# Batch 0's attention of the state rows as a separate pass between batches 2 and 3 of a fused attention, MLP and MoE kernel

## The chip, the cores and the metric

The kernel runs on one NeuronCore of a Trainium2 chip. The metric is the device time of one execution in microseconds (us). The engines are TensorE (PE, matrix products), VectorE (DVE), ScalarE (ACT), GpSimd (POOL) and SyncE (SP, whose queue issues most DMA transfers and DMA transposes). Each engine works its own queue of instructions in order, so an instruction that waits holds up everything behind it on that engine.

## What is computed

Three stages follow each other. The first is an attention between 512 token rows and 32 state rows, for 8 batches and 8 heads, in both directions. The results of a batch (512 + 32 rows of 8 x 64 columns) are laid side by side to 4608 tokens of 512 columns, and these go through an MLP and then through a mixture of 8 experts of which each token takes one.

```python
# x: [8, 8, 512, 64], state: [8, 8, 32, 64]   (batch, head, row, column)
scores  = x @ state.T / 8
xread   = softmax(scores) @ state              # the 512 token rows
scores2 = state @ x.T / 8
sread   = softmax(scores2) @ x                 # the 32 state rows
x = concatenate([xread, sread], rows)          # 4608 x 512

h = x @ w_in                                   # 512 x 2048
x = (maximum(h, 0) ** 2) @ w_out               # 2048 x 512

expert = argmax(x_normed @ emb_normed.T / tau) # one of 8
out = gate * (maximum(x @ w1[expert], 0) @ w2[expert])   # 512 x 1024 x 512
```

`w_in` and `w_out` come as fp64 and are turned into fp32 on the chip; all other inputs and the output are fp32.

## The kernel before

**Precision.** Most fp32 products are made of three fp16 products: each factor is split into a high part and the rest (`split`, `splits`: a scaled copy on ACT, L331, and a subtraction on DVE, L317). A scale for each matrix comes first, from sums of squares. Batch 0's score products, and the first products with `w_in`, are taken in fp32, before any scale is known.

**Work units.** The token rows of batch b are two units of 256 tokens, u = 2b and 2b + 1, and all state rows together are the last unit, u = 16. `w_in` has eight blocks of columns, c = 0 to 7. The MLP's first product uses that xread is a weighted sum of state rows: for each batch, `state_w` (L674, for batch 0 `first_state_w`) makes `sw` = state x `w_in` once, in four steps k = 0 to 3 of two PSUM banks `S0` and `S1` (pool `ps_s`, one of each), and `up1` multiplies the transposed attention weights `aT` with `sw` into a tile `u` of PSUM (L1388 to L1390, twelve products a unit and block with two units side by side; two buffers). `hidden` reads `u` on ACT (L1341) and goes on to `g`, and `down1` multiplies `g` with `w_out` into `d` (L1472 to L1474).

**The token side of the attention.** `attention(b)` waits for x and the state of its batch, for the end of batch b - 1, and for the tile of the splits. It takes squares (L463, L465), makes scales and splits of x and the state, and the scores. `weigher` then makes the softmax, writes it in halves (the cast L544 on ACT, the subtraction on DVE) and asks SP for the transpose into `aT` (L553), one for each unit. Batch 0 has functions of its own: `first_attention`, `first_scores` (fp32 products, L604) and `first_scale` (the scale of x).

**The state side.** `state_side(b)` makes the scores of the state rows (L756; fp32 products for batch 0, three fp16 products for the others), the maxima (L763), two exps (L768), the splits of the exps into `he`, a transpose of `he` through SP (L779), two splits of `xS` (L331), 48 closing products (L800 to L802), and the two halves `x8_h` (L810, two instructions) and `x8_l` of its columns of unit 16. It ends with `ev("att", b)`, on which batch b + 1 waits. For batch 0 it is started by `first_scale`, and it has two waits of its own: for the scale of x (`"first sx"`), and at L772 for a step of the weights' preparation:

```python
GATE_S = ('wosq', 3)
...
        if b == 0:
            yield ev(*GATE_S)
```

**Buffers and loads.** x comes twice per batch: as `xT` (columns first, for scores) and as `xS` (rows first, for the closing products). Both use one buffer of 1 MB (`xf_slots`), the state has one buffer (`st_slots`), the halves one (`xhl_slots`), and the exps with their transposes one (`eb_slots`). All four are single, and lie in the tiles that the trace calls `xx`, `stt`, `xx` and `he`. `loader` brings the batches in turn, each load as soon as the buffer is free:

```python
        yield from load_x(0, 1)
        for b in range(1, B):
            yield from load_st(b)
            yield from load_x(b, 0)
            yield from load_x(b, 1)
```

**What sets the order.** No scheduler runs on the chip. At build time a planner (`Plan`) holds a list of threads (Python generators such as `attention(b)`, `state_side(b)`, `loader`), each with a priority. A thread yields an engine and an estimated duration, an event, or a buffer. The planner takes the thread that can start first (with the priority, a lower number first, where they tie) and writes its instructions into the engine's queue. So a change in a thread, in a wait or in a priority shifts the order of all engines behind it.

**The early stage.** While batches 0 and 1 go through attention, the weights `w_in` and `w_out` are loaded, turned into fp32 (first step on ACT, L908), squared (ACT L940, L999) and split (`wi`, ACT L986; `wo_t`, ACT L1047). Later, while the MLP runs over batches 1 to 7, the experts' weights are loaded, split and stored as `w_d`, 2 MB for each load of the MoE stage. That stage starts behind the MLP (L1688 loads, L1782 to L1784 first products).

Of the kernel before, what the change touches and what calls it, by code (L numbers as in the profile page):

```python
# [41 lines left out]
BW = DFF // NB  # L42
GATE_S = ('wosq', 3)
BLOCKS = [(kind, 2 * k + i) for k in range(NB // 2) for kind in "io" for i in range(2)]
# [9 lines left out]
PRIO_A1 = 1.25  # L54
PRIO_S0 = 1.1
XE = 2
SMALL = 2
# [188 lines left out]
def moe_kernel(  # L246
# [154 lines left out]
    def ev(*key):  # L401
        return evs.setdefault(key, Ev(plan))
# [19 lines left out]
    def load_st(b):  # L422
        yield st_slots
        stt = att.tile([128, 4, 64], F32, name="stt")
        t = yield from load(stt, stT[b], 128 * 1024)
        st_t[b] = stt
        ev("st", b).set(t)

    def load_x(b, which):
        yield xf_slots  # L430
        t = xf_v
        xf_t[b, which] = t
        if b or which:
            ev("x", b, which).set((yield from load(t, (xT, xS)[which][b], 1 << 20)))
        else:
            for i in range(2):
                q = slice(256 * i, 256 * i + 256)
                ev("first x", i).set((yield from load(t[:, :, q], xT[0][:, :, q], 1 << 19)))

    def loader():  # L440
        yield ev("raw", LOADER)
        yield from load_x(0, 1)
        for b in range(1, B):
            yield from load_st(b)
            yield from load_x(b, 0)
            yield from load_x(b, 1)
# [5 lines left out]
    def attention(b):  # L452
        yield ev("x", b, 0)
        yield ev("st", b)
        xf, stt = xf_t.pop((b, 0)), st_t.pop(b)
        yield ev("att", b - 1)
        yield xhl_slots
# [106 lines left out]
    def first_attention():  # L564

        yield ev("st", 0)
        stt = st_t.pop(0)
        yield xhl_slots
        xh, xl = halves_tile()
        ss = small.tile([128, 3], F32, name="ss")  # L570
        yield act(256)
        nc.scalar.activation(out=xl.bitcast(BF16)[:, :, :64], in_=stt, func=AF.Square, accum_out=ss[:, 2:3])
        yield t_slots
        p = ps_t.tile([128, 512], F32, name="t")
        yield "pe", 0.2
        mm(p[:, 2:3], lhsT=one32, rhs=ss[:, 2:3], start=True, stop=True)
        mm(p[:, 256:512], lhsT=oneb, rhs=xl.bitcast(BF16)[:, :, :64], start=True, stop=True)
        for t in range(2):
            plan.add(first_scores(t, xh, xl, stt), 0.4 + 0.1 * t)
        plan.add(first_scale(ss, stt), 0.95)  # L580
        v = small.tile([128, 2], F32, name="sv")[:, 0:1]
        yield tiny(4)
        V.tensor_scalar(out=v, in0=p[:, 2:3], scalar1=FLOOR, scalar2=None, op0=ALU.max)
        pow2(sx[:, 1:2], isx[:, 1:2], v, 204)
        yield sth_slots
        sthl = att.tile([128, 2, 4, 64], F16, name="sthl")
        stf = sthl.rearrange("p a c n -> p (a c n)").bitcast(F32).rearrange("p (c n) -> p c n", c=4)
        yield dve2(256)
        V.tensor_scalar(out=stf, in0=stt, scalar1=sx[:, 1:2], scalar2=float(2.0 ** -14), op0=ALU.mult, op1=ALU.mult)
        plan.add(first_state_w(stf), 0.6)  # L590
        plan.add(group_bound(0, p), 0.7)

    def first_scores(t, xh, xl, stt):
# [5 lines left out]
        Sp, k_h = ps_u.tile([128, 512], F32, name="u").rearrange("p (a n) -> p a n", a=2), u_slots.last()  # L599
        yield "pe", 3.4  # L600
        for a in range(2):
# [8 lines left out]
    def first_scale(ss, stt):  # L610

        for t in range(2):
            yield ev("scored", t)
        xf = xf_t.pop((0, 0))
        plan.add(state_side(0, ((stt, xf),), eighth), PRIO_S0)
        for i in range(2):
# [3 lines left out]
            nc.scalar.activation(out=jk, in_=xf[:, 2 * i:2 * i + 2], func=AF.Square, accum_out=ss[:, i:i + 1])  # L620
            pjk_slots.release()
        at = plan.now()
        yield t_slots
# [9 lines left out]
        pow2(sx[:, 0:1], isx[:, 0:1], v, 204)  # L633
        ev("first sx").set()
        for C in range(2):
            yield ev("ST", 0, C)
        xf_slots.release()
# [101 lines left out]
    def state_side(b, pairs, scl):  # L739
# [9 lines left out]
        for C in range(2):  # L749
            yield t_slots  # L750
            plan.cur[2] = max(at, plan.now())
            p = ps_t.tile([128, 512], F32, name="t")
            yield "pe", 0.8 if b else 1.7
            for n, (a, x) in enumerate(pairs):
# [6 lines left out]
        for C, p in enumerate(ps):  # L761
# [8 lines left out]
            t_slots.release()  # L770
        if b == 0:
            yield ev(*GATE_S)  # L772
        yield tiny(3)
# [7 lines left out]
        yield ev("x", b, 1)  # L781
        if b == 0:
            yield ev("first sx")
        xs = xf_t.pop((b, 1))
        yield xhl_slots
        xsh, xsl = halves_tile()
        sxb = sx[:, 2 * b:2 * b + 1]
        yield from splits([(xsh[:, q], xsl[:, q], xs[:, q], sxb) for q in (slice(0, 2), slice(2, 4))], 1024)
# [16 lines left out]
        pov = po[:, 0:256].rearrange("p (c i n) -> p c i n", c=4, i=2)  # L805
        ns = slice(b * NS, b * NS + NS)
        qs = [(i, slice(64 * i, 64 * i + 64)) for i in range(2)]
# [1061 lines left out]
    def start():  # L1869
# [6 lines left out]
        for b in range(1, B):  # L1876
            plan.add(attention(b), 1.15 if b == 1 else PRIO_A1)
        plan.add(loader(), 1)
# [51 lines left out]
```

## Time and profile before

| | us |
|---|---|
| median of 3 runs | 1085.97 (1083.8 to 1086.14) |
| the profiled execution | 1084.85 |
| its span, from the first to the last instruction | 1083.1 |
| PE busy | 1040.1 (96% of the span) |
| DVE busy | 666.7 (62%) |
| ACT busy | 590.3 (55%) |
| POOL busy | 121.6 (11%) |

The granted clock of PE is 0.987 of its full rate as a mean over the span. The MoE stage's first products start at 689.52 us. To read such a profile: busy shares say which engine is full over the whole span, but stages differ, so a table of stretches comes next. The list of waits says what ended the idle time in front of an instruction. A timeline gives the start of each instruction on one engine, its duration, and in brackets the idle time before it with what ended it. Starts of instructions that follow each other at once lie closer together than the durations, since they overlap in the engine.

### The profile page before, as it was taken

Reading aid. Unit: us, or ns where it says so; the run is one execution under the profiler, and the core shown is the slowest. Engines: PE = TensorE matmul, PEld = TensorE weight load, DVE = VectorE, ACT = ScalarE, POOL = GpSimd, SP = SyncE. Lnnn points to the kernel's source line nnn. Section 1 sums busy time; section 2 is a strip of 40 time slices with the busy share of each in tenths; the row PEclk is TensorE's granted clock in tenths of the full one; section 3 lists DMA queues with packets and bytes.
Section 4 is the critical chain, followed back from the end, with each engine's and each line's share of the span. In section 5 each row is a group of like instructions: output and inputs, shape, how many; then the busy total and the mean of one; then the engine's idle time right before and its main releaser. Section 6 shows DMA issues by size and latency. Waiting matters only on the chain. (4 is left out here: it accounts for less than half of the span.)

```text
span 1083.1 us, 26144 instructions
## 1 busy us (share of the span) xinstructions
PE 1040.1 (96%) x10521; PEld 669.9 (62%) x10521; DVE 666.7 (62%) x1817; ACT 590.3 (55%) x990; POOL 121.6 (11%) x149
## 2 busy tenths in 40 slices
PE   5989999999999999999999999999999999999988
PEld 4445555565565665655656566677767667776764
DVE  6779888878878788788876864465233222222222
ACT  6999988878878789778768773111111101011110
POOL 0000000102001001010020200321121122121101
PEclk9889999999999999999999999999999999999999
DMA  9854567676674867667377677935986766875690
GB/s 298 326 169 146 124 199 168 187 196 175 167 204 149 184 163 233 165 196 215 79 224 223 213 252 270 230 89 148 301 236 167 214 174 198 230 226 151 207 294 30
DMA packets 161311, 211.73 MB, mean 195 GB/s; under 512 B 112225, under 2 KB 115041, under 8 KB 155938
## 3 DMA queue, kind: packets, MB, share of 16 engines
q1 hardware_dynamic: 152434, 182.86, 58.9%
q0 software_dynamic: 8320, 27.08, 7.8%
q8 instruction: 84, 1.38, 0.5%
q14 instruction: 41, 0.34, 0.1%
q10 hardware_dynamic: 432, 0.08, 0.0%
HBM read 257.92 MB, written 51.68 MB: 286 GB/s over the span
## 5 line engine op out<-in xcount | busy, mean ns | idle before, releaser
L1738 ACT ACTIVATE r<-u 128x512 f32<-128x512 f32 x70 | 41.8, 597 | 327.6 <-PE u L1784 300.2
L1474 PE MATMUL d<-wo_t,g 128*128 128x512 f16 x480 | 181.9, 379 | 1.4 <-DVE g L1360 1.4
L1472 PE MATMUL d<-wo_t,g 128*128 128x512 f16 x480 | 181.9, 379 | 0.8 <-DVE g L1358 0.8
L1473 PE MATMUL d<-wo_t,g 128*128 128x512 f16 x480 | 181.9, 379 | 0.0
L1388 PE MATMUL u<-aT,sw 128*128 128x256 f16 x512 | 141.2, 276 | 13.0 <-ACT sw L666 5.5
L1390 PE MATMUL u<-aT,sw 128*128 128x256 f16 x512 | 140.9, 275 | 0.7 <-DVE sw L317 0.7
L1389 PE MATMUL u<-aT,sw 128*128 128x256 f16 x512 | 141.0, 275 | 0.2 <-issue 0.2
L1741 DVE CAST hh<-r 128x512 f16<-128x512 f32 x70 | 30.1, 430 | 139.4 <-ACT r L1738 137.8
L1341 ACT ACTIVATE r<-u,cg 128x512 f32<-128x512 f32 x120 | 81.8, 684 | 50.7 <-PE u L1390 32.3
L1752 DVE TENSOR_SCALAR o<-d,rec,wo_t 128x512 f32<-128x512 f32 x35 | 28.3, 810 | 109.8 <-PE d L1807 103.0
L1314 POOL DMA_INDIRECT rec_d<-rec,pi x34 | 38.1, 1119 | 483.0 <-DVE g L1360 111.2
L1807 PEld LDWEIGHTS <-hh 128*128 128x128 f16 (+1 forms) x688 | 54.9, 103 | 58.0 <-issue 2.0
L1360 DVE TENSOR_TENSOR g<-r,g 128x512 f16<-128x512 f32 x120 | 82.2, 688 | 7.6 <-ACT r L1355 6.1
L1474 PEld LDWEIGHTS <-g 128*128 128x128 f16 x480 | 47.0, 98 | 58.7 <-DVE g L1360 1.9
L1783 PE MATMUL u<-xes,stage 128*128 128x128 f16 x448 | 76.0, 219 | 0.0
L1784 PE MATMUL u<-xes,stage 128*128 128x128 f16 x448 | 76.0, 219 | 0.0
L1782 PE MATMUL u<-xes,stage 128*128 128x128 f16 x448 | 76.0, 219 | 0.0
L1355 ACT ACTIVATE r<-r 128x512 f32<-128x512 f32 x120 | 74.6, 626 | 1.2
L1472 PEld LDWEIGHTS <-g 128*128 128x128 f16 x480 | 47.1, 98 | 45.4 <-DVE g L1358 1.3
L1388 PEld LDWEIGHTS <-sw 128*128 128x128 f16 x512 | 51.3, 100 | 37.6 <-issue 17.3
L1473 PEld LDWEIGHTS <-g 128*128 128x128 f16 x480 | 47.0, 98 | 44.0
L1782 PE MATMUL u<-xes,xx 128*128 128x128 f16 x416 | 70.5, 219 | 0.0
(331 smaller groups left out, 2610.1 us busy)
## 6 DMA issues: line engine op xcount, KB each, us to landing
w_d<-he SPq DMA_DIRECT2D x128, 256.0 KB
g<-w_d SPq DMA_DIRECT2D x16, 2048.0 KB
wo_t<-w_d SPq DMA_DIRECT2D x16, 2048.0 KB
stage<-w_d SPq DMA_DIRECT2D x14, 2048.0 KB
he<-w_d SPq DMA_DIRECT2D x14, 2048.0 KB
xx<-w_d SPq DMA_DIRECT2D x13, 2048.0 KB
sw<-w_d SPq DMA_DIRECT2D x13, 2048.0 KB
stage<-in_w_dram SPq DMA_DIRECT2D x21, 1024.0 KB
```

The source lines that it names most:

```text
L1341: nc.scalar.activation(out=r, in_=ps, func=AF.Relu, scale=cg[:, g:g + 1] if u >= F32U else cgq[:, c:c + 1])
L1355: nc.scalar.activation(out=r, in_=r, func=AF.Square)
L1360: V.tensor_tensor(out=gl, in0=r, in1=gh, op=ALU.subtract)
L1388: mm(o, lhsT=hl[:, i, 0, fs], rhs=aT[:, i, :], start=i == 0, stop=False)
L1389: mm(o, lhsT=hl[:, i, 0, fs], rhs=aT[:, 2 + i, :], start=False, stop=False)
L1390: mm(o, lhsT=hl[:, i, 1, fs], rhs=aT[:, i, :], start=False, stop=i == 1)
L1472: mm(ps, lhsT=g_h[:, f, ts], rhs=w[:, 0, :], start=f == 0, stop=False)
L1473: mm(ps, lhsT=g_h[:, f, ts], rhs=w[:, 1, :], start=False, stop=False)
L1474: mm(ps, lhsT=g_l[:, f, ts], rhs=w[:, 0, :], start=False, stop=f == KF - 1)
L1782: mm(p[:, j, xs], lhsT=w[:, 0, k, fs], rhs=xe[:, k, xs], start=k == 0, stop=False)
L1783: mm(p[:, j, xs], lhsT=w[:, 0, k, fs], rhs=xe[:, 4 + k, xs], start=False, stop=False)
L1784: mm(p[:, j, xs], lhsT=w[:, 1, k, fs], rhs=xe[:, k, xs], start=False, stop=k == 3)
```

## The change

The state side of batch 0 no longer runs with the rest of batch 0. A new thread `late_side` runs it as a pass of its own with the number B = 8, at the fourth place of a list ATT = (0, 1, 2, 8, 3, ..., 7). Its parts:

- `loader` goes through ATT. `xT` and the state of batch 0 are loaded a second time for the pass (index `b % B`), and `xS` of batch 0 is loaded then and not early. The first load behind batch 0's `xT` is now the state and `xT` of batch 1.
- `first_scale` frees x and the state of batch 0 once the squares are made, and starts no state side. A new event `"stf"` says that the scaled state has been written, since the state's buffer may go only then.
- `attention(b)` waits for the pass ahead of it in ATT. Batch 1 waits for no other batch. Its priority goes from 1.15 to 1.0. Batch 3 now waits for the late pass, and the late pass for batch 2.
- The two waits that `state_side` had for batch 0 go away. The late pass still uses fp32 score products (1.7 us in the planner instead of 0.8).
- The planner's estimate for the first score products goes from 3.4 to 3.2 us.

```diff
-GATE_S = ('wosq', 3)
+ATT = (0, 1, 2, B, 3, 4, 5, 6, 7)
...
-        t = yield from load(stt, stT[b], 128 * 1024)
+        t = yield from load(stt, stT[b % B], 128 * 1024)
...
-            ev("x", b, which).set((yield from load(t, (xT, xS)[which][b], 1 << 20)))
+            ev("x", b, which).set((yield from load(t, (xT, xS)[which][b % B], 1 << 20)))
...
         yield ev("raw", LOADER)
-        yield from load_x(0, 1)
-        for b in range(1, B):
+        for b in ATT[1:]:
             yield from load_st(b)
             yield from load_x(b, 0)
             yield from load_x(b, 1)
...
     def attention(b):
...
-        yield ev("att", b - 1)
+        if b > 1:
+            yield ev("att", ATT[ATT.index(b) - 1])
...
         V.tensor_scalar(out=stf, in0=stt, scalar1=sx[:, 1:2], scalar2=float(2.0 ** -14), op0=ALU.mult, op1=ALU.mult)
+        ev("stf").set()
...
-        yield "pe", 3.4
+        yield "pe", 3.2
...
     def first_scale(ss, stt):
...
         for t in range(2):
             yield ev("scored", t)
+        yield ev("stf")
+        st_slots.release()
         xf = xf_t.pop((0, 0))
-        plan.add(state_side(0, ((stt, xf),), eighth), PRIO_S0)
...
             pjk_slots.release()
+        xf_slots.release()
...
         ev("first sx").set()
+
+    def late_side():
+
+        yield ev("x", B, 0)
+        yield ev("st", B)
+        xf, stt = xf_t.pop((B, 0)), st_t.pop(B)
+        yield ev("att", ATT[ATT.index(B) - 1])
+        plan.add(state_side(B, ((stt, xf),), eighth), PRIO_S0)
         for C in range(2):
-            yield ev("ST", 0, C)
+            yield ev("ST", B, C)
         xf_slots.release()
         st_slots.release()
...
     def state_side(b, pairs, scl):
...
-            yield "pe", 0.8 if b else 1.7
+            yield "pe", 0.8 if b < B else 1.7
...
-        if b == 0:
-            yield ev(*GATE_S)
...
-        if b == 0:
-            yield ev("first sx")
...
         for b in range(1, B):
-            plan.add(attention(b), 1.15 if b == 1 else PRIO_A1)
+            plan.add(attention(b), 1.0 if b == 1 else PRIO_A1)
+        plan.add(late_side(), PRIO_A1)
```

Lines behind the new function carry a number 7 to 11 higher in the changed kernel (L666 becomes L677, L756 becomes L767, L1341 becomes L1348).

What the planner makes of it is shown at three places. The first is SP's queue from the last `w_in` load to the first transpose into `aT` of batch 1 (`aT<-xx`); `he<-he` is the transpose of a state side, `xx` the buffer of x, `stage` a buffer of raw weights. Before:

```order
L339 DMA stage<-in_w_in_dram 128x4x1023
L779 DMA_TRANSPOSE he<-he 128x16x128
L339 DMA xx<-in_xT_dram 128x2048
L339 DMA he<-in_w_out_dram 128x2x2048
L339 DMA stage<-in_w_out_dram 128x2x2047
L339 DMA stage<-in_w_dram 128x2x1024 x2
L339 DMA xx<-in_xS_dram 128x2048
L339 DMA stt<-in_stT_dram 128x256
L553 DMA_TRANSPOSE aT<-xx 128x8x128
L779 DMA_TRANSPOSE he<-he 128x16x128
```

And now:

```order
L339 DMA stage<-in_w_in_dram 128x4x1023
L339 DMA he<-in_w_out_dram 128x2x2048
L339 DMA stage<-in_w_out_dram 128x2x2047
L339 DMA stage<-in_w_dram 128x2x1024 x2
L339 DMA xx<-in_xS_dram 128x2048
L339 DMA stt<-in_stT_dram 128x256
L788 DMA_TRANSPOSE he<-he 128x16x128
L553 DMA_TRANSPOSE aT<-xx 128x8x128
```

The transpose and the load of `xT` have left the upper part (`xT` of batch 1 is now asked for further up, where `xS` of batch 0 stood), and batch 1's transpose of `he` stands ahead of its first `aT`.

The second place is ACT's queue at the third step of batch 0's `sw` (L666 before, L677 now). L463 takes the squares of batch 1's x; L908 (L915) begins the turn of weights into fp32, L940 and L999 (L947, L1006) take their squares, L986 splits `wi`. Before:

```order
L999 ACTIVATE pjk,woacc<-wo_t 128x1024
L986 ACTIVATE wi<-wi,swi 128x1024
L810 ACTIVATE x_h<-t 64x4x32 x2
L999 ACTIVATE pjk,woacc<-wo_t 128x1024
L1341 ACTIVATE r<-u,cgq 128x512
L666 ACTIVATE sw<-S_511,swi 128x512
L1345 ACTIVATE g<-r 128x2x2x128
L463 ACTIVATE xx,ss<-xx 128x1024
L666 ACTIVATE sw<-S_512,swi 128x512
L463 ACTIVATE xx,ss<-xx 128x1024
```

And now:

```order
L915 ACTIVATE rec_129<-wo_t 128x1024
L915 ACTIVATE rec_128<-stage 128x1024
L915 ACTIVATE rec_129<-stage 128x1024
L1006 ACTIVATE pjk,woacc<-wo_t 128x1024
L1348 ACTIVATE r<-u,cgq 128x512
L1006 ACTIVATE pjk,woacc<-wo_t 128x1024
L1352 ACTIVATE g<-r 128x2x2x128
L677 ACTIVATE sw<-S_482,swi 128x512
L947 ACTIVATE pjk<-wi 128x1024
L677 ACTIVATE sw<-S_483,swi 128x512
```

The pair that writes `x_h` is gone, and the squares of batch 1's x, which stood around the second of these reads, now stand ten and eight rows above the first row shown.

The third place is PE's queue behind batch 2's closing products, at the end of a group of `sw` products (`S` from `wi` and `sthl`). L1292 and L1293 (L1299, L1300) belong to the expert choice of earlier tokens. Before:

```order
L692 LDWEIGHTS sthl
L692 MATMUL S_2096<-wi,sthl 32x512
L692 LDWEIGHTS sthl
L692 MATMUL S_2097<-wi,sthl 32x512
L1292 LDWEIGHTS cs_94
L1292 MATMUL t<-oh,cs_94 128x32
L1293 LDWEIGHTS one_96
L1293 MATMUL t<-cum,one_96 128x32
L1388 LDWEIGHTS sw
```

And now:

```order
L703 LDWEIGHTS sthl
L703 MATMUL S_1954<-wi,sthl 32x512
L703 LDWEIGHTS sthl
L703 MATMUL S_1955<-wi,sthl 32x512
L767 MATMUL t<-xx,stt 64x512 x2
L1299 LDWEIGHTS cs_94
L1299 MATMUL t<-oh,cs_94 128x32
L1300 LDWEIGHTS one_96
L1300 MATMUL t<-cum,one_96 128x32
L1395 LDWEIGHTS sw
```

The first half of the late pass's fp32 score products (`t` from `xx` and `stt`) stands between a group of `sw` products and the next `u` products.

## Rows read from the trace of the kernel before

**Rows 1.** Table by stage: stretch, us, busy time per engine, granted clock, DMA share, GB/s.

```profile
60.00:80.00 20.00, 14.82 (x137) 8.88 (x136) 13.72 (x40) 17.85 (x31) 0.37 (x2) 0.74 0.39 153
100.00:110.00 10.00, 7.45 (x54) 3.62 (x54) 9.26 (x25) 10.00 (x18) 0.00 (x0) 0.83 0.42 79
110.00:180.00 70.00, 70.00 (x512) 38.48 (x510) 59.55 (x143) 60.36 (x100) 0.00 (x0) 1.00 0.60 153
180.00:280.00 100.00, 97.27 (x899) 58.60 (x897) 82.79 (x236) 84.21 (x149) 12.73 (x16) 1.00 0.68 191
```

The engines in these rows are PE, PE's weight loads, DVE, ACT and POOL.

**Rows 2.** Waits of PE, 0 to 200: us in total, times, longest.

```profile
PE S L657 <- DVE sw L317: 4.8, 2, 3.9
PE u L1388 <- DMA aT<-xx: 2.6, 1, 2.6
```

**Rows 3.** Timeline of PE at u = 2: start, us, instruction, idle before.

```profile
103.60 0.27 PE L1390 MATMUL u<-aT,sw 128*128 128x256 f16 x1
106.43 0.40 PE L1388 MATMUL u<-aT,sw 128*128 128x256 f16 x1 [2.55 <-DMA aT<-xx]
...
107.82 1.48 PE L692 MATMUL S<-wi,sthl 64*32 64x512 f16 x24
```

**Rows 4.** Timeline of PE: batch 0's state rows, and later products at full clock.

```profile
21.25 1.08 PE L756 MATMUL t<-xx,stt 128*64 128x512 f32 x4
...
61.05 0.19 PE L800 MATMUL t<-he,xx 128*128 128x64 f16 x1
...
62.45 0.27 PE L1388 MATMUL u<-aT,sw 128*128 128x256 f16 x1
...
167.24 0.27 PE L1390 MATMUL u<-aT,sw 128*128 128x256 f16 x1
...
170.03 0.84 PE L692 MATMUL S<-wi,sthl 64*32 64x512 f16 x24
```

**Rows 5.** Timeline of ACT: batch 0's state side, and the last `sw` reads.

```profile
38.38 0.76 ACT L768 ACTIVATE he<-t,mt,eighth 128x512 f32<-128x512 f32 x1
...
46.77 0.72 ACT L331 ACTIVATE he<-he,rt 128x512 f16<-128x512 f32 x1
47.38 0.63 ACT L1345 ACTIVATE g<-r 128x512 f32<-128x512 f32 x1
...
52.21 1.16 ACT L331 ACTIVATE xx<-xx,sx 128x1024 f16<-128x1024 f32 x1
...
63.08 0.56 ACT L810 ACTIVATE x_h<-t 64x128 f16<-64x128 f32 x2
...
75.66 0.69 ACT L1341 ACTIVATE r<-u,cgq 128x512 f32<-128x512 f32 x1 [2.09 <-PE u L1390]
...
79.33 0.68 ACT L666 ACTIVATE sw<-S,swi 128x512 f16<-128x512 f32 x1
```

**Rows 6.** Timelines of ACT and SP at batch 1's first transposes (SPq: SP's queue).

```profile
101.95 0.61 ACT L544 CAST xx<-xx 128x512 f16<-128x512 f32 x1
...
103.31 1.23 SPq L553 DMA_TRANSPOSE aT<-xx  x1
...
105.33 1.93 SPq L779 DMA_TRANSPOSE he<-he  x1
```

**Rows 7.** Timelines of SP, PE and ACT: two loads of the next x.

```profile
178.94 0.34 SPq L339 DMA_DIRECT2D xx<-in_xT_dram  x1
...
180.95 0.19 PE L800 MATMUL t<-he,xx 128*128 128x64 f16 x1
...
467.95 0.34 SPq L339 DMA_DIRECT2D xx<-in_xT_dram  x1
...
474.56 1.06 ACT L463 ACTIVATE xx<-xx 128x1024 bf16<-128x1024 f32 x1 [2.44 <-DMA xx<-in_xT_dram]
```

**Rows 8.** Timelines of SP and PE: the MoE stage's first load and products.

```profile
653.34 0.36 SPq L1688 DMA_DIRECT2D stage<-w_d  x1
...
689.52 0.22 PE L1782 MATMUL u<-xes,stage 128*128 128x128 f16 x1
```

More of the change, by code (lines that the diff above doesn't have):

```diff
@@ L786, in state_side @@
         xsh, xsl = halves_tile()
-        sxb = sx[:, 2 * b:2 * b + 1]
+        sxb = sx[:, 2 * (b % B):2 * (b % B) + 1]
         yield from splits([(xsh[:, q], xsl[:, q], xs[:, q], sxb) for q in (slice(0, 2), slice(2, 4))], 1024)
@@ L805, in state_side @@
         pov = po[:, 0:256].rearrange("p (c i n) -> p c i n", c=4, i=2)
-        ns = slice(b * NS, b * NS + NS)
+        ns = slice(b % B * NS, b % B * NS + NS)
         qs = [(i, slice(64 * i, 64 * i + 64)) for i in range(2)]
```

## The prediction

> **What bounds the kernel now.** The table by stage comes first [rows 1]: TensorE (PE) is idle 5.2 of 20 us in 60:80 and 2.6 of 10 us in 100:110, and both stretches run at a reduced granted clock (0.74 and 0.83), while ScalarE (ACT) is busy 17.9 of 20 and then 10.0 of 10 us. From 110 on PE is busy 70.0 of 70 us and then 97.3 of 100. So up to about 105 us the kernel is held by ACT's queue, and from 110 on by PE's own work. What is saved early therefore reaches the end, and PE work that is put behind 110 us is paid in full. The waits come second and name the early stops [rows 2]: two of 4.8 us together in front of the last `sw` products of batch 0 (the S banks are single, so these products wait for VectorE (DVE) to read the ones before), and 2.6 us for the first transposed weights `aT` of batch 1. The timeline of PE comes third, at that place [rows 3]. It is the gate of this case: the first product of u = 2 starts at 106.43 after its wait, and runs with the 24 behind it at the lower of the clock's two levels (1.2 GHz): 0.40 us a product where 0.27 is usual.
>
> **What leaves the early stage.** On ACT: two exps of L768, two splits of `he` (L331), two of x (L331) and the pair that writes `x_h` (L810). Their rows [rows 5] last 0.76, 0.72, 1.16 and 0.56 (both) us, and in ACT's unbroken queue the next one starts 0.1 us ahead of an end (46.77 + 0.72 against 47.38): 0.61 and 1.04 from start to start. The exps keep 0.75, since a read of the accumulator follows each, and the pair 0.59. That makes 1.5 + 1.2 + 2.1 + 0.6 = 5.4 us. On PE: two groups of fp32 products (1.08 us at the full clock) and 48 small products that take 1.4 us (61.05 to 62.45) [rows 4]. These stood in front of stops that PE had anyway, so taking them away gains PE nothing there. About 6 us leave DVE too, but ACT is the fuller of the two. On the DMA queue xT of batch 1 takes the place of xS of batch 0, 1 MB for 1 MB, so the weights behind it come no later.
>
> **When the first product of u = 2 comes.** I follow ACT's queue in the new order, priced from start to start. Up to the read of the last `sw` of batch 0 (L666 at 79.33 before [rows 5]) it loses the 5.4 us above and one L1341 (0.6), and gains two `wi` splits that now stand earlier (2 x 1.04, as the splits of x of the same shape): 3.9 us less. ACT's wait of 2.09 us at 75.66 [rows 5] comes from PE, which stood at the S banks [rows 2]. The `sw` that held them now follows sooner, so I let that wait go too. From there to the first cast of batch 1 (L544, 101.95 before [rows 6]) the new queue is 1.2 us longer: one each of L331, L532 and L697 more and one L1345 less; two `wi` splits leave it and two `wo` splits of the same shape come. L544 then starts at 101.95 - 3.9 - 2.1 + 1.2 = 97.2.
>
> Before, `aT` was asked for 1.36 us after that start (103.31) and its first product began 3.1 us after the ask (106.43) [rows 3, 6]. Alone it would start at 97.2 + 1.36 + 3.1 = 101.7. But the new order puts the transpose of `he` ahead of `aT` on SP, where it stood behind it. Its source is ready one DVE instruction (0.7 us) sooner, so it is asked for at 97.9 and holds SP for 1.93 us [rows 6]. `aT` goes out at 99.8, and the product starts at **102.9**. The bounds: 101.7, as if `he` cost nothing, and 106.0, if all of `he` must land first (97.9 + 1.9 + 3.1) and `aT` takes its 3.1 after that. I take 102.9, since the rows show the hold on SP and nothing that says one transfer waits for all of the one ahead. The u buffer that this product needs comes free at about the same time: it is read by the fifteenth L1341, which the same sum over the new queue brings to 101 to 102 us.
>
> The Trainium skill, page "DMA: Bandwidth & Descriptors", section "Latency and other measured facts", speaks against the swap on SP: it gives 261 GB/s as the effective rate of a DMA transpose whose middle dimension is not contiguous. An estimate from that page puts the 0.5 MB of `he` at 2.0 us; added to the ask at 99.8 it starts the product at 104.9, and the sum would end 2 us later, at 1085.7. No row of before shows the rate itself.
>
> **What PE has done and what it owes.** At that product PE has two groups of 24 `sw` products of batch 1 behind it that stood behind the product before: 2 x 0.84 = 1.7 us ahead [rows 4]. It owes the state rows of batch 0: 2 x 1.08 + 1.4 = 3.6 us at the full clock, behind 110 us where nothing hides them. The lower clock at 106 to 109 cost 1.2 us: 0.6 on six products (1.3 where 0.65 is usual) and 0.6 on the 24 (1.48 against 0.84) [rows 3, 4]. Whether it comes back depends on how long PE still stands ahead of u = 2. In the new order PE has little left to do after 100 us, so a stop of up to 2.5 us remains. I take half, 0.6, with 0 and 1.2 as ends.
>
> The Trainium skill, page "TensorE: Matmul & The Clock Gate", section "Part 1: The HAM clock gate (the "warmup" mystery)", says that the throttled level is the default and that activity releases it. By that rule a shortened stop keeps the clock up, the 1.2 us come back whole, and the time is that of the second case below.
>
> **The moved pass itself.** ACT and DVE have about 15% free behind 110 us (60.4 and 59.6 busy of 70, then 84.2 and 82.8 of 100) [rows 1], which hides 5.4 and 6 us over the 100 us that the pass spans. If that cover were gone, 5.4 us would be paid once. The second load of x and the state is 1.1 MB; the DMA share there is 0.60 to 0.68 [rows 1], so it hides too, if it comes in time (third rival). The last batch's state rows end about seven `u` tiles later in PE's order, and the expert weights' last buffers with them. The fetch of the first expert's weights goes out at 653.34 and its first product is at 689.52 [rows 8]: 36 us for a load of 2 MB, so a delay of some 20 us stays hidden.
>
> **The sum.** 106.43 - 102.9 = 3.5, + 1.7 + 0.6 - 3.6 = 2.2 us. The profiled execution took 1084.85 (its span 1083.1 and 1.75 around it); less 2.2 is 1082.6. The median of the runs, 1085.97, lies 1.1 above it, so the forecast is **1083.7**. By the bounds: 4.7 + 1.7 + 1.2 - 3.6 = 4.0 gained at best (1082.0), and 0.4 + 1.7 - 3.6 = 1.5 lost at worst (1087.5).
>
> **Rivals.**
> First, the forecast: `aT` comes sooner, 3.6 us are owed, and 2.2 remain. Chance 0.40; its own spread is 1082.5 to 1085.
> Second, the clock stays at 2.4 GHz and `he` does not hold `aT`: 1082.0. For it: the gate moves by almost 5 us. Against it: ACT stays full, so PE may still stand there. Chance 0.20.
> Third, on the other side: **the moved fp32 products stop PE's queue.** In PE's queue the first of them stands 5.6 us of work behind the start of batch 2's closing products: these 1.4, six `u` products 0.65, twelve `d` products 2.7, 24 `sw` products 0.84 [rows 4]. Its x can only be asked for when batch 2 has split its own xS out of the same buffer. Before, the ask for the next x came 2.0 us ahead of those closing products (178.94 and 180.95 [rows 7]), so the load has about 7.6 us. Where ACT stood waiting for such a load it took 6.6 (467.95 to 474.56 [rows 7]). Against this rival: 1 us to spare. For it: expert loads and stores share the DMA engines. If the load takes 12.2 us, somewhat under twice that, PE stands 4.6 us, everything behind on PE waits with it, and the time is 1088.3. It costs from 7.6 us on, and is a loss over 0.2% from about 12. SP would stand too, since its next xS waits for those products. Chance 0.14.
> Fourth, the gate moves less: `aT` waits for the whole of `he`, or DVE is as full as ACT and holds L544. The product starts at 105 to 106, and the time is 1086 to 1087.5. Chance 0.18.
> Fifth, the change does not do what it says: batch 1 does not go ahead, because its split waits for the last scales of `wi`, which the weight loads set, and not for batch 0. Then only the debt is left, 3.6 - 1.7 = 1.9 us, and the time is 1087.9. Against it: the last weights were asked for behind the transpose that now leaves the early stage. Chance 0.08.
>
> **How the numbers follow.** A difference under 0.2% (2.2 us) is about what a measurement of this kernel cannot tell from no change. The forecast case gives somewhat over half its chance to faster (0.22) and the rest to the same (0.18). The second is faster (0.20). The fourth is nearly all the same (0.16), with 0.01 on either side. The third is slower (0.13) but for a part (0.01). The fifth lies just inside the same (0.06) or over (0.02). Rounded: faster 0.44, same 0.40, slower 0.16. The range 1081.5 to 1087.6 takes in the bounds of the first, second and fourth case and leaves out most of the third and a part of the fifth.
>
> **What would show it.** The first product of u = 2 between 101.7 and 106 instead of 106.43, the first cast of batch 1 near 97, and a higher clock in 100:110. Ahead of it, stops at the S banks shorter than 4.8 us together. Behind 110 us PE as full as before, with two fp32 groups of 1.08 us among its `u` and `d` products and no wait on x in front of them. I am wrong if PE's idle time behind 110 us grows by more than a microsecond, or if ACT reaches the fifteenth L1341 no earlier than 105.

## The result, and the profile after

The changed kernel is slower: 1094.65 us (median of 6 runs, 1091.82 to 1098.02) against 1085.47 in the same comparison, a ratio of 1.0098 with a 95% interval of 1.0077 to 1.0119. Two later comparisons gave 1.0102 (1.0072 to 1.0131) and 1.0109 (1.0087 to 1.0131). The forecast was 1083.7 with a range up to 1087.6. The profiled execution of the changed kernel took 1093.9 us.

The page of after, its span and its line on PE:

```profile
span 1092.1 us, 26131 instructions
...
PE 1038.5 (95%) x10521; PEld 668.1 (61%) x10521; DVE 667.1 (61%) x1813; ACT 593.6 (54%) x994; POOL 121.9 (11%) x149
```

Before, PE was busy 1040.1 of 1083.1 us and idle 43.0. Now it is busy 1038.5 of 1092.1 and idle 53.6. So the 9.0 us of the span are 10.6 us more idle time of PE and 1.6 us less busy time. PE does the same 10521 products in both; the smaller busy time goes with a higher granted clock (0.998 as a mean, before 0.987). What was lost was lost in stops, not in work.

The table by stage of after, in the stretches of [rows 1]:

```profile
60.00:80.00 20.00, 17.60 (x114) 9.82 (x112) 17.21 (x38) 19.64 (x31) 2.49 (x2) 1.00 0.41 148
100.00:110.00 10.00, 6.76 (x37) 4.25 (x31) 7.98 (x22) 8.72 (x18) 0.00 (x0) 0.83 0.64 88
110.00:180.00 70.00, 70.00 (x557) 39.25 (x556) 60.86 (x152) 58.12 (x95) 0.00 (x0) 1.00 0.60 166
180.00:280.00 100.00, 94.47 (x849) 55.99 (x848) 78.79 (x213) 80.89 (x142) 10.76 (x16) 1.00 0.71 197
```

In 60:80 PE has 2.8 us more busy time, at 1.00 of the clock instead of 0.74. In 100:110 it still stops, and the clock is 0.83 again. Behind 180 it is idle 5.5 us of 100 where it was idle 2.7.

Where the idle time lies is read from the same table cut otherwise: stretch, its us, then PE's busy us (idle is the difference). Before:

```profile
0.00:110.00 110.00, 88.65 (x642) 52.57 (x643) 86.45 (x208) 97.61 (x146) 2.67 (x17) 0.89 0.70 233
...
180.00:220.00 40.00, 38.67 (x351) 23.13 (x349) 31.87 (x87) 33.30 (x59) 5.54 (x8) 1.00 0.73 202
...
540.00:600.00 60.00, 59.25 (x453) 35.29 (x452) 44.51 (x143) 47.26 (x78) 6.16 (x8) 1.00 0.75 225
600.00:740.00 140.00, 137.57 (x1209) 92.66 (x1208) 86.11 (x327) 55.08 (x91) 24.66 (x27) 1.00 0.67 198
```

And after:

```profile
0.00:110.00 110.00, 85.94 (x616) 50.62 (x617) 86.50 (x206) 97.99 (x147) 4.80 (x17) 0.98 0.68 221
...
180.00:220.00 40.00, 35.56 (x308) 20.85 (x307) 29.03 (x80) 33.53 (x60) 5.08 (x8) 1.00 0.92 257
...
540.00:600.00 60.00, 56.87 (x461) 33.33 (x459) 42.47 (x111) 47.07 (x83) 4.96 (x8) 1.00 0.69 199
600.00:740.00 140.00, 136.27 (x1158) 90.80 (x1157) 88.10 (x342) 63.13 (x105) 23.95 (x25) 1.00 0.67 198
```

Idle time grows by 2.7 us up to 110, by 3.1 in 180:220, by 2.4 in 540:600 and by 1.3 in 600:740. The other 1.1 of the 10.6 is spread over the rest. Behind 110 us that is 7.9 us more idle time, where the prediction named more than one microsecond as a sign of being wrong. Two further profiles of the changed kernel (e5, e17) and one of the kernel before (e6) give nearly the same four: 23.4 to 24.1 us idle against 21.4, 4.0 to 4.5 against 1.3, 3.0 to 3.2 against 0.8, and 2.8 to 4.1 against 2.4.

The gate, in the timelines of ACT, SP and PE of after (rows as in [rows 3, 6]):

```profile
97.30 0.63 ACT L544 CAST xx<-xx 128x512 f16<-128x512 f32 x1
...
97.83 1.80 SPq L788 DMA_TRANSPOSE he<-he  x1
99.68 1.96 SPq L553 DMA_TRANSPOSE aT<-xx  x1
...
104.80 0.40 PE L1395 MATMUL u<-aT,sw 128*128 128x256 f16 x1 [3.24 <-DMA aT<-xx]
```

The cast comes 4.65 us sooner than before, the product of u = 2 only 1.63. From the ask for `aT` to its first product it takes 5.1 us where it took 3.1. Ahead of that product PE has the same products behind it as before, but for 48 more `sw` products and the 8 fp32 and 48 closing products of the pass, which it still owes.

The late pass, in the timelines of SP and PE of after (the ask for its x, its fp32 products, its transpose of `he`, its closing products):

```profile
171.32 0.34 SPq L339 DMA_DIRECT2D xx<-in_xT_dram  x1
...
177.65 1.08 PE L767 MATMUL t<-xx,stt 128*64 128x512 f32 x4
...
196.31 5.91 SPq L788 DMA_TRANSPOSE he<-he  x1
...
205.13 0.20 PE L807 MATMUL t<-he,xx 128*128 128x64 f16 x1 [2.76 <-DVE g L1367]
```

The x came in time: no wait stands in front of the fp32 products. The closing products wait 2.76 us. The row names DVE, but the transpose of `he` held SP until 202.2, and in e5's profile the same wait (2.87 us, at 202.47) is put down to it, as in e18's (2.57 us). In five profiles with this order (after, e5, e15, e17, e18) the closing products start 2.9 us behind the end of that hold, whatever the row names. The window 180:220 holds one more stop of 1.55 us, for a scale of expert weights; in the kernel before there are 1.3 us of other waits in it.

At 564 to 567 PE stops inside the closing products of the last batch, for nothing that the profile shows ("issue"):

```profile
564.71 0.19 PE L808 MATMUL t<-he,xx 128*128 128x64 f16 x1 [0.27 <-issue]
565.44 0.19 PE L809 MATMUL t<-he,xx 128*128 128x64 f16 x1 [0.55 <-issue]
566.86 0.19 PE L808 MATMUL t<-he,xx 128*128 128x64 f16 x1 [1.20 <-issue]
```

### The profile page after: what moved, and what is told of

The parts are those of the page before. It is cut to its first block, busy times and chain, and to the rows that moved or that the text cites. A ratio compares the mean times of both kernels' runs of the same rounds, so it can differ in the third digit from the quotient of the medians.

```text
span 1092.1 us, 26131 instructions
## 1 busy us (share of the span) xinstructions
PE 1038.5 (95%) x10521; PEld 668.1 (61%) x10521; DVE 667.1 (61%) x1813; ACT 593.6 (54%) x994; POOL 121.9 (11%) x149
## 5 line engine op out<-in xcount | busy, mean ns | idle before, releaser
L1348 ACT ACTIVATE r<-u,cg 128x512 f32<-128x512 f32 x120 | 82.0, 684 | 51.5 <-PE u L1397 29.5
L1321 POOL DMA_INDIRECT rec_d<-rec,pi x34 | 35.5, 1044 | 517.3 <-ACT r L1348 134.9
```

The source lines that it names most:

```text
L1348: nc.scalar.activation(out=r, in_=ps, func=AF.Relu, scale=cg[:, g:g + 1] if u >= F32U else cgq[:, c:c + 1])
```

## The experiments

The comparisons fall into two groups by the kernel before's own time: 1083 to 1085 us (the first comparison, e5 to e8, e17 and e18) and 1073.5 to 1075 us (the other twelve). Each of the comparisons behind the first ran on a chip of its own, so group and chip can't be told apart. Only ratios to the kernel before of the same comparison are set side by side. The changed kernel itself was only measured in the first group.

At least half of the 10 us between the groups lies in the experts' stage, where the edits change nothing by intent. The same table for one stretch of it, in the profiles of before, after and e15 (second group):

```profile
740.00:1040.00 300.00, 294.68 (x4143) 216.72 (x4141) 85.49 (x158) 32.85 (x55) 56.00 (x54) 1.00 0.72 211
...
740.00:1040.00 300.00, 294.49 (x4113) 216.20 (x4111) 90.76 (x193) 32.85 (x55) 56.98 (x55) 1.00 0.69 205
...
740.00:1040.00 300.00, 300.00 (x4215) 220.80 (x4213) 93.47 (x196) 33.44 (x56) 56.60 (x54) 1.00 0.73 217
```

PE is idle 5.3 and 5.5 us in the first two and not at all in the third (3.7 to 5.6 us in all eight profiles of the first group, at most 0.7 in the twelve of the second). Within the first group the changed kernel loses nothing to the kernel before there: all of its 10.6 us more idle time lies ahead of 740.

**Is it the pass? Take it out, or mend its two stops (e1 to e4).**

e1 leaves the late pass out; batch 0's state rows are then not computed, and `fill_rows` puts copies of batch 1's in their place:

```diff
-ATT = (0, 1, 2, B, 3, 4, 5, 6, 7)
+ATT = (0, 1, 2, 3, 4, 5, 6, 7)
...
-        plan.add(late_side(), PRIO_A1)
+        plan.add(fill_rows(), PRIO_A1)
```

> The changed kernel without the late pass: batch 0's state rows are left out, and their columns of unit 16 are a copy of batch 1's, made on POOL. Theory A, the pass itself makes the loss (3.6 us of PE work, the 2.76 us stop of PE in front of its closing products at 205 us, and what follows from them): the whole loss goes, 1083 to 1085 us against 1094.7 for the changed kernel, PE's lag at 110 us as in the changed kernel. Theory B, the new order of the early stage and of the rest makes it: only the 3.6 and the 2.8 go, 1088 us or more.

Measured: 1.0024 (1.0012 to 1.0037). Without the pass, with 3.6 us less work, the kernel is still slower than the kernel before, so the 3.6 us and the stop at 205 us are not the story by themselves (theory B). PE loses the gain at the handover to the experts:

```profile
693.55 0.28 PE L1250 MATMUL t<-en,xr 128*128 128x16 f16 x4 [5.28 <-DMA xr<-rec]
```

e2 puts batch 1's `aT` ahead of its `he`:

```diff
+        if b == 1:
+            yield ev("asked", 2)
         yield "sp", 0.06
         nc.sync.dma_start_transpose(e, eb[:, 1024:2048].bitcast(F16))
```

> The changed kernel, with batch 1's transpose of he asked for only behind its first aT, as in the kernel before. If the transpose of he ahead of it is what made aT land 5.1 us after it was asked for (3.1 in the kernel before), the first product of u = 2 starts near 102.3 to 102.9 us instead of 104.8 and the time falls by 1 to 2 us to about 1093. If aT was late for another reason (the weight loads), it starts at 104 or later and the time stays at 1094.7.

Measured: 1.0013 (0.9997 to 1.0028). The product starts at 102.91, as expected, but the ratio lies 0.85% under the changed kernel's, far more than the 1 to 2 us that were expected. And from the ask for `aT` (98.17) it is still 4.7 us, though `he` now follows 1.3 us behind; in e9, with the same two asks, it is 5.1 again. Before, with `he` 2.0 us behind, it was 3.1. So which of the two is asked for first decides little. That two transposes delay each other while both are under way fits these rows; no run has the one without the other.

e3 moves the late pass's closing products back:

```diff
-        turned = plan.dma(1 << 19) + 1.0
+        turned = plan.dma(1 << 19) + (8.0 if b == B else 1.0)
```

> The changed kernel, with the planner told that the late pass's transpose of he takes 7 us longer, so that its closing products stand further back in PE's queue. Theory A: the 2.76 us stop in front of them at 205 us goes, and some 3 us of the loss with it: about 1092. Theory B: it goes, but another stop takes its place behind, and the time stays within 1.5 us of 1094.7.

Measured: 0.9991 (0.9978 to 1.0005), the kernel before's time and 1.1% under the changed kernel's ratio, far more than the stop that the edit aimed at. That stop even stays in another form: 3.08 us for a transposed record at 199.6, and 3.1 us idle in 180:220. What went lies behind: PE is idle 0.9 us in 540:600 and 1.2 in 600:740 (3.1 and 3.7 in the changed kernel).

e4 is the kernel before with the change's two planner constants, cut from two places:

```diff
-        yield "pe", 3.4
+        yield "pe", 3.2
...
-            plan.add(attention(b), 1.15 if b == 1 else PRIO_A1)
+            plan.add(attention(b), 1.0 if b == 1 else PRIO_A1)
```

> The kernel before with only the two planner constants of the change (batch 1's priority 1.15 to 1.0, the estimate 3.4 to 3.2). Theory A: within 2 us of the kernel before (1085.5). Theory B, the planner's order is so finely balanced that any shift of it costs: 3 us or more slower, with stops in places that have nothing to do with batch 0.

Measured: 1.0014 (1.0001 to 1.0027). The constants alone don't make the loss (theory A).

**The changed kernel again, and small shifts of its order (e5 to e8).** e5 is the changed kernel, e6 the kernel before. e7 is the changed kernel with the edit of e4 undone; e8 changes one priority:

```diff
-        plan.add(state_side(b, pairs, scl), 1.28)
+        plan.add(state_side(b, pairs, scl), 1.0 if b == 7 else 1.28)
```

> The changed kernel once more, on the chip of this call and beside its runs of the kernel before. Theory A (the pass and the stop behind it make the loss): 1.007 to 1.012 of the kernel before, as measured first. Theory B (the loss of 0.98% is the change in that one comparison, made of stops that fall otherwise on another chip, as near relatives of the kernel stand at 0.999 to 1.001): 0.999 to 1.004.

> The kernel before, for a profile from the chip of this call, since the profile read ahead of the prediction and those of the first four experiments can't be laid side by side in time (the same kernel took 1085.5 us there and 1074.6 here). Theory A: its first product of u = 2 at 106 to 107 us and its last product d at 688 to 690, as before; what differs between the chips lies in the stage of the experts.

> The changed kernel with the two planner constants of the kernel before (priority 1.15 of batch 1, estimate 3.4). aT of batch 1 then stands ahead of its transpose of he on SP, and the late pass lies at the same place in PE's queue. Theory A: as the changed kernel, within 2 us, less 1 to 2 for the earlier aT. Theory B (the loss comes from stops behind 300 us that hang on the planner's exact order): anywhere within 4 us of the kernel before, and at least 4 us faster than the changed kernel.

> The changed kernel, with the state side of the last batch alone at a higher priority: the order is the changed kernel's up to about 490 us, and the last batch's closing products stand further ahead in PE's queue. Theory A (what is lost is lost by 210 us): no change, within 1.5 us of the changed kernel. Theory B (3 us at 563 to 567 and 4 us at the handover to the experts are lost because the last batch's state rows end 27 us later): 3 to 6 us faster than the changed kernel, and its loads of expert weights go out by 660 us.

Measured in one comparison: e5 1.0102 (1.0072 to 1.0131), e6 1.0005 (0.9985 to 1.0025), e7 1.0026 (1.0009 to 1.0043), e8 1.0055 (1.0033 to 1.0077). e7 has the whole late pass and is 6.6 us faster than the changed kernel. Its table by stage:

```profile
180.00:220.00 40.00, 38.90 (x330) 22.48 (x329) 30.95 (x81) 35.17 (x65) 6.25 (x8) 1.00 0.86 267
...
540.00:600.00 60.00, 57.98 (x497) 35.09 (x496) 45.77 (x147) 47.01 (x80) 5.07 (x8) 0.97 0.65 200
600.00:740.00 140.00, 137.43 (x1204) 92.49 (x1204) 85.53 (x322) 59.14 (x99) 24.27 (x26) 1.00 0.66 197
```

It is idle 1.1, 2.0 and 2.6 us where e5 is idle 4.5, 3.0 and 2.8: 3.4 us less around the late pass, 1.0 less at the last batch, 0.2 less at the handover. The two profiled executions lie 4.0 us apart. The late pass's closing products have no wait in front of them. e8 is the changed kernel up to about 490 us. It gains 3.1 us by the medians, and the stops inside the last batch's closing products don't stand in its profile. So theory B held for e7 and, at its lower end, for e8: the loss follows the order, and not the pass alone.

**Is it the change at all? Nudge the kernel before (e9 to e12).** e10 and e11 are the kernel before with one number each, which is meant for nothing; e9 joins the edits of e2 and e3; e12 is e1 with the priority of e8. The edits of e10 and e11:

```diff
-        turned = plan.dma(1 << 19) + 1.0
+        turned = plan.dma(1 << 19) + (12.0 if b == 2 else 1.0)
```

```diff
-        plan.add(state_side(b, pairs, scl), 1.28)
+        plan.add(state_side(b, pairs, scl), 1.0 if b == 2 else 1.28)
```

> The changed kernel with both edits of the second and third experiment: batch 1's aT ahead of its transpose of he, and the late pass's closing products further back. Theory A (the early gate and the one stop at 205 us carry the result, and add up): PE's lag at 220 us is 5 us less than the changed kernel's, and the time 0.994 to 0.998 of the kernel before. Theory B (from 220 us on each new order meets its own stops, which cost 0 to 10 us): the lag at 220 us is as low, but the time lies anywhere from 0.995 to 1.006.

> A control without the change: the kernel before, with the planner told that batch 2's transpose of he takes 11 us longer. Nothing is moved by intent; the order differs from about 185 us on. Theory A: within 0.15% of the kernel before. Theory B: 0.2 to 0.8% slower, as the kernel before happens to have few stops at the handover and any other order behind 200 us has more.

> A second control without the change: the kernel before, with the state side of batch 2 at a higher priority in the planner. Theory A: within 0.15% of the kernel before. Theory B: 0.2 to 0.8% slower, with its stops in other places than the first control's.

> The changed kernel without the late pass (batch 0's state rows left out, their columns a copy of batch 1's), with the state side of the last batch at a higher priority as in the eighth experiment. Its early and middle part are those of the first experiment, which was 3.5 us ahead at 660 us and lost some 9 us at the handover, 5.3 of them in one wait for a gathered record's transpose. Theory A (the pass is free or costs up to 3 us, and the first experiment lost its gain at the handover alone): that wait is shorter and the time is 0.995 to 0.999 of the kernel before. Theory B (what is saved ahead of the handover is given back there in any order, since the expert weights set its time): 1.001 to 1.004 again.

Measured: e9 1.001 (0.9992 to 1.0029), e10 1.008 (1.0052 to 1.0107), e11 1.011 (1.0082 to 1.0139), e12 0.992 (0.9899 to 0.994). The two controls have no part of the change and lose about as much as the changed kernel does in the other group; e11 lies above the 0.2 to 0.8% that were expected. With e4 (0.14%), all three shifts of the kernel before are slower than it, so its own order seems to be one with few stops; with three, no more can be said. Each control has its own stops; e10's largest, and two of e11's that the kernel before doesn't have:

```profile
698.40 0.27 PE L1235 MATMUL t<-en,xr 128*128 128x16 f16 x4 [6.03 <-DMA xr<-rec]
```

```profile
197.02 0.58 PE L692 MATMUL S<-wi,sthl 64*32 64x512 f16 x1 [2.02 <-DVE sw L317]
...
688.69 0.26 PE L1782 MATMUL u<-xes,stage 128*128 128x128 f16 x1 [4.84 <-DMA xes<-rec]
```

e12 differs from e1 by one priority, which acts on the last batch alone, and is 1.0% faster, more than either theory had: the wait of 5.28 us is not in its profile.

e9 and e12 also price the pass. The pages give e9 a span of 1071.6 with PE busy 1034.0, and e12 1063.4 with 1029.0: 5.0 us of work and 3.2 us of idle time. The list of waits behind 690 us puts that idle time in one place; e9's only row there is

```profile
PE u L1793 <- issue: 3.3, 1, 3.3
```

and e12 has none. It lies in the experts' stage, where the copied rows of e12 may also go to other experts. So in this pair of orders a pass whose stops are mended costs its work, 3.6 us by the rows and 5.0 here at most, and no stop that can be put down to it.

**What makes the stop at the handover? (e13 to e16, e18).** In e1 and e10, which lose 5 to 6 us there, two things stand otherwise than in the kernel before: PE has the experts' first products ahead of the last products `d`, and the third load of expert weights goes out late. SP's timeline in e10, and in the kernel before:

```profile
679.05 0.35 SPq L1688 DMA_DIRECT2D xx<-w_d  x1
...
683.68 6.82 SPq L1225 DMA_TRANSPOSE xr<-rec  x1
```

```profile
663.27 0.35 SPq L1688 DMA_DIRECT2D xx<-w_d  x1
...
682.27 1.23 SPq L1225 DMA_TRANSPOSE xr<-rec  x1
```

e13, e14 and e15 set PE's order alone, in e1's kernel, in e10's and in the changed one. e16 and e18 move the load, in e1's kernel and in the changed one (in e16 48 rows of PE's order move with it). The two edits:

```diff
     def up2(t, m2):
+        if t == 0:
+            yield ev("moe1")
```

```diff
-                        yield ev("moe1") if name == "w2" else ev("cum", NXT - 1)
+                        if name == "w2":
+                            yield ev("moe1")
```

> The kernel of the first experiment (no late pass, batch 0's state rows left out) with one more wait in the planner: the experts' first products stand behind the last products d in PE's queue. All before the handover is as in the first experiment (1.0024). Theory C, this order makes the stop of 5 us at the handover: the stop goes and the time is 0.992 to 0.997 of the kernel before, as in the twelfth. Theory D, the late third load of expert weights makes it: the stop stays, 1.001 to 1.003.

> The first control (the kernel before, nudged at batch 2, without the change: 1.008) with the same wait for the last products d. Theory C: the 6 us wait for a transposed record at 698 us goes, and the time is 0.999 to 1.003. Theory D: 1.006 to 1.009.

> The changed kernel (1.010) with the same wait for the last products d. Theory C: 2 to 4 us less, 1.006 to 1.008, since it lost 4 to 5 us at the handover where the kernel before loses 2.4; the rest (3 us at 195 to 206, 4 at 555 to 567) stays. Theory D: no change, 1.009 to 1.011.

> The kernel of the first experiment with the third load of expert weights asked for directly behind the second, at about 653 us instead of 675; PE's order at the handover stays as it was but for 48 rows. Theory C: the stop stays, 1.000 to 1.003. Theory D: it goes, 0.992 to 0.997.

> The changed kernel with the third load of expert weights asked for directly behind the second, as in the sixteenth run. Theory D (that load, when it is late, makes the stops at the handover): 3 to 5 us faster than the changed kernel of the same call. If the handover's loss in this kernel is not the load's: within 1.5 us of it.

Measured: e13 1.0031 (1.0012 to 1.005), e14 1.0075 (1.0046 to 1.0104), e15 1.0047 (1.0032 to 1.0063), e16 0.9911 (0.9892 to 0.9931), e18 1.0117 (1.0088 to 1.0145). PE's order changes nothing in e13 and e14: the waits for the transposed record are 3.99 and 8.07 us. The load decides in e16: asked for 12.7 us sooner, it takes 1.1% away, and no wait for the record stands at the handover. In e1 the load goes out at 675.29 and the transpose of the record at 678.25, where it holds SP for 7.12 us; in e16 the load goes out at 662.62 and that transpose at 685.77, for 1.23 us. PE's idle time in 600:740 falls from 8.8 to 0.7 us: 5.3 is the wait for the record, and 3.5 are two waits for `g` that stand ahead of e1's load, so they come from the rest of the order and not from the load's landing. (The profiled execution of e16 took 1073.4 us where its median is 1065.2, and has such a wait elsewhere, 5.58 us at 562.85.) So the stop of 5.28 us in e1 comes from a small transpose that goes out behind a 2 MB load; that e10's has the same cause is read from its rows alone, since e14 leaves its load late.

In the changed kernel itself this is not the cause. e18 asks for the load at 668.46 instead of 693 and is no faster than e17 (1095.9 and 1095.63): a wait of 2.31 us for other transposed records comes in its place.

e17 is the changed kernel beside e18:

> The changed kernel beside the eighteenth run. If its profile shows stops put down to issue, as the first two did (2 to 3 us ahead of 690 us, 9 to 10 behind): 1.008 to 1.012 of the kernel before. If it shows none, the stops of issue were a part of the loss where they came up, and the ratio is 1.004 to 1.008, near the fifteenth run (1.0047), which has the same order up to the handover.

Measured: 1.0109 (1.0087 to 1.0131), with stops of issue, 3.4 us ahead of 690 and 9.4 behind. e15 has the same order up to the handover, was measured in the second group, shows 1.1 us idle in 540:600, none of it and none ahead of 690 put down to issue, and stands at 1.0047, under both of its theories. That the changed kernel would lose about half as much in the second group is likely from this, and was not measured. In the first group its three profiles have 11.8 to 12.7 us of stops of issue in all, and the two of the kernel before 9.0 and 5.6; so a part of its loss, 3 to 7 us by these profiles, belongs to the order and the group together.

## Why the prediction was wrong

**ACT's queue: right.** The cast was forecast at 97.2 and came at 97.30 (96.1 to 97.3 in three profiles); `he` was asked for at 97.83 (97.9) and `aT` at 99.68 (99.8). Following one full queue, start to start, gave the order's effect. The last tenths are luck: the third step's `sw` read, 79.33 before, came at 73.84 where the sum has 73.3, and the way from there to the cast took 0.4 us less than the sum has.

**The first product of u = 2: mis-sized.** The step "`aT` goes out at 99.8, and the product starts at 102.9" took 3.1 us for the transfer. It took 5.1, which takes 1.9 us from the gate's 3.5. The forecast kept SP's hold and took the transfer itself as undisturbed. That the other transpose delayed it is the likely cause, from before, e2 and e9, and not shown by itself. The Trainium skill, page "DMA: Bandwidth & Descriptors", section "Latency and other measured facts", gave 104.9 by the estimate in the prediction; the trace agrees with 104.80. The number agrees; the way to it is not borne out, since e9 asks for `aT` first and it takes as long.

**The clock: nothing came back in this profile.** PE still stopped 3.24 us, and the twelve products behind the stop ran 0.40 to 0.42 us each; this term was forecast at 0.6, and its lower end, 0, held. But it is no sure term of the change. The changed kernel in e5 stops 3.28 us at this place and runs the twelve at 0.27 to 0.28 us each, and the kernel before in e6 stops 2.56 us and does so too (granted clock of 100:110 1.00 in both). The prediction took it for the kernel's from one execution. With 1.63 for the gate, the same 1.7 for the `sw` products and 3.6 owed, the sum gives a loss of 0.3 us and not a gain of 2.2. That alone is a time of 1086.3, "the same".

**The moved pass: the third rival at another place.** The x was in time (asked for at 171.32, used at 177.65 without a wait). The stop came 20 us behind the second half of those products, at the closing products, for the pass's own transpose of `he`, which took 8.8 us from its ask in a stretch with a DMA share of 0.92. The prediction had priced the pass's loads and not its transpose. Cost: 2.1 to 2.9 us in the five profiles with this order (after, e5, e15, e17, e18); e7 shows that another order hides it.

**The order behind 200 us: the step that failed.** The forecast's sentence "What is saved early therefore reaches the end, and PE work that is put behind 110 us is paid in full" takes it that the rest of the program stays as it is. It does not: the planner writes another order from there on, and this order has its own stops. By subtraction (9.2 us between the medians, less 0.3 and 2.8) some 6 us are of that kind, the stops of issue among them. e7 gives 6.6 us back with the same work and another order, beside e5 in one comparison. e10 and e11 show the size with no part of the change in them, 0.8 and 1.1%; e2, e3, e7 and e9 have the change's pass and stand at 0.999 to 1.003, e8 and e15 at 1.0055 and 1.0047. So the change doesn't force the loss, and what decides the result is where the stops of the new order fall. What the change is worth by intent is known from the terms alone (a loss of 0.3 us, 3.1 with the stop at the closing products): no time of one order can show so little where orders differ by 1%. The range left this out, and with it most of the chance of a loss.

**The handover: a cover that was not one.** The prediction hid "a delay of some 20 us" of the first load of expert weights. In the changed kernel the first load went out 13 us later (666) and the third 31 us later (694.5 against 663.3), and 1.3 us more were lost there. In e1 the stop that goes with the third load's place took 5.3.

What stays open: how the changed kernel's idle time behind 220 us divides among single causes, and how much of it would be there on another chip. e8 and e15 each take a part away, e18 none, and no single edit of the handover gave all of it back.

No kernel that does all the work was clearly faster than the kernel before: e3 came nearest, 0.9991 with an interval that holds 1.

## What to carry to other kernels

Where a planner or scheduler writes the order, price a change by its own terms, and then add a spread for the new order: measure that spread by nudging a number that is meant for nothing, before any gain or loss below it is put down to the edit. In the order of the changed kernel, look at the joints between stages (which large load stands ahead of which small transfer on a queue), also where the change has no business. And a moved step brings its transposes with it: each has to land beside what is under way there.

## What the runs showed of the hardware

- Stops that are put down to issue belong to some runs of the same program and not to others. Behind 690 us they are 8.1 us in the profile of the kernel before and 8.9 in that of the changed kernel, in many short stops; in the second group of comparisons there is one of 1.3 to 3.5 us (3.3 in e9) or none. The second group's kernel before is 10 us faster, and the idle time in 740:1040, 5.3 us against none, is about half of that. What makes these stops, the traces don't show.
- The clock behind one and the same stop differs between executions of one program: products of 0.42 us behind a stop of 3.24 us in the first profile of the changed kernel, of 0.27 us behind 3.28 us in e5's.
- A transpose holds SP for 1.23 us when little is under way (`aT` at 103.31 before), and for 5.9 (`he` at 196.31), 6.8 and 10.0 us (`xr` behind a 2 MB load, e10 and e16) when much is. In e16 the hold of 10 us cost nothing, since nothing waited for that record yet.
- The page's name for a releaser can be wrong by an engine: the 2.76 us at 205 us stood under DVE in one profile, and under the DMA in another of the same program (e5).
